# Retention and a gated feed-forward layer on one core: the same operations in another order

## The chip, the cores and the metric

The kernel runs on one core of a Trainium2 chip. The core has a matrix engine (PE, with its weight loads shown apart as PEld), a vector engine (DVE), a scalar engine (ACT), GpSimd (POOL) and a queue engine (SP), each working through its own list of instructions in order. They meet through semaphores. The metric is the time of one execution on the device in microseconds (us); runs are compared by their medians.

## The reference

Four sequences of 768 tokens, eight heads of 64. For each head a state is decayed by a fixed factor and takes up k times v at every token; the output is q times the state. What the eight heads give for a token is one row of 512, which is divided by its root mean square, multiplied by a gain, and goes through a gated layer with 1536 hidden units.

```python
gamma = 1.0 - 2.0 ** (-5.0 - np.arange(H))
for t in range(S):
    state = gamma * state + k[t] (outer) v[t]
    y[t] = q[t] @ state / sqrt(D)
x = y.transpose(0, 2, 1, 3).reshape(B * S, H * D)
xn = x / sqrt(mean(x * x) + 1e-6) * rms_g
out = (silu(xn @ w_gate) * (xn @ w_val)) @ w_out
```

## The kernel before, in words

The tokens of each sequence are cut into six chunks c of 128; b is one of the four batches. Inside a chunk the recurrence is written as matmuls: scores k times q for all pairs of tokens, multiplied by a mask that holds the decay and the causal order, times v, and for c > 0 also q times the state that the chunks before left. The four batches of a chunk are 512 tokens, and these go through the feed-forward layer together.

Nothing in the kernel is scheduled by the framework. A string, ORDER (lines 17 to 100), names every operation in the order in which it is written out, and the loop at its end (lines 600 to 604) calls one small function for each word. A word is an operation, its indices, after @ the engine (D, A, P, S for DVE, ACT, POOL, SP), and after / the PSUM banks that it writes (eight banks, 0 to 7). Each engine carries out its own instructions in this order; an instruction that waits holds up all that stand behind it on its engine. The words that matter here:

- Lq, Lk, Lv load a tile of 128 tokens (load, L314; for chunk 0 through POOL in an arrangement of eight tokens a row, L312). Through POOL the transfer also turns float32 into bfloat16; through SP it does not, and Cq, Ck, V make the bfloat16 tile later. wg, wv, wo load weights through POOL (L323, L330). These transfers of POOL use one software queue and eight semaphores in turn, so a POOL transfer waits for the one that was issued eight places before it. Loads of chunk 2 wait for the last piece of wo.
- Tq, Tk transpose with PE (L366, L371) and Eq, Ek copy the result out; from chunk 2 on tq, tk transpose by a DMA of SP (L387) instead. ident and pick are the matrices for this. J (L510) turns a transposed k of chunk 0 back.
- mk0, mk1, vd, yd, yt are exponentials on ACT that make masks and decays; mc (L282) makes the two halves of chunk 1's mask on POOL from the causal triangle.
- A are the scores (L403), M0 and M1 their products with the mask (DVE, L426), Y the output (L441, and L445 for the state's part), S its squares (ACT, L458), R the power -1/2 on POOL (L468, L470), N the normalised row xn (DVE, L482), X and XE its transposition (PE L495 with a copy, or SP's DMA L501 from chunk 2 on).
- D scales k (L517), K multiplies k and v (L526), U adds to the state in float32 (L534), B copies it to bfloat16 on POOL (st_b, L541), which the next chunk's Y reads.
- g and v are groups of the feed-forward layer's first matmuls (L549; c, blocks n0 to n1, batches b0 to b1), s the silu on ACT (L559), h the product on DVE (L567), d and, for the last tile, e the second matmuls (L574, L596), o the copy to SBUF, st the store by SP.
- G and GE spread the gain over the partitions (g_bc), tab loads ACT's table for silu, hot and H are idle matmuls (L234, L240) that only keep PE busy.

Buffers come from rings: a tile's slot is given again when its readers are done.

Of the kernel before, what the change touches and what calls it, by code (L numbers as in the profile page):

```python
# [27 lines left out]
s.0.3.4.0.3 XE.0.3@A g.0.0.4.3.4/6 s.0.2.3.0.3 h.0.0.2.1.2 g.0.4.6.3.4/4 wv.9.12 g.0.4.5.0.3/7 v.0.4.6.3.4/5
v.0.2.3.0.3/3 U.0.1@D s.0.4.6.3.4 Ek.1.1@A h.0.3.4.0.3 g.0.5.6.0.3/0 s.0.4.5.0.3 h.0.4.6.3.4 mc.0@P mc.1@P
v.0.4.5.0.3/5 v.0.0.4.3.4/7 h.0.2.3.0.3 Tk.1.2/1 g.0.6.7.0.4/4 Ek.1.2@A Lv.1.2@P h.0.4.5.0.3 g.0.7.8.0.4/2  # L30
Lv.1.0@P wo.0.4 Tq.1.2/1 s.0.5.6.0.3 s.0.7.8.0.4 Eq.1.2@D B.0.1 g.0.8.9.0.4/3 A.1.2/51 v.0.5.6.0.3/0 M1.1.2
wo.4.8 wo.8.12 s.0.0.4.3.4 v.0.7.8.0.4/2 h.0.0.4.3.4 h.0.5.6.0.3 h.0.7.8.0.4 Lk.1.3@P D.1.2@P Lk.2.0@S
v.0.6.7.0.4/7 Tk.1.0/0 M0.1.2 Lk.2.3@S Tq.1.0/6 v.0.8.9.0.4/1 s.0.6.7.0.4 Ek.1.0@A Eq.1.0@D h.0.6.7.0.4
s.0.8.9.0.4 Lq.2.1@S A.1.0/6042 M0.1.1 M1.1.0 B.0.2 M1.1.1 g.0.11.12.0.4/3 g.0.9.10.0.4/5 g.0.10.11.0.4/4
s.0.11.12.0.4 K.1.1/3 Y.1.1/0 s.0.10.11.0.4 h.0.8.9.0.4 S.1.1 U.1.1@D M0.1.0 v.0.9.10.0.4/2 v.0.10.11.0.4/3
R.1.1 v.0.11.12.0.4/4 s.0.9.10.0.4 K.0.3/7 h.0.9.10.0.4 D.1.0@P U.0.3@A Y.1.2/2 S.1.2 h.0.10.11.0.4 Y.1.0/3
N.1.1 h.0.11.12.0.4 Lq.1.3@P S.1.0 B.0.3 Lq.2.0@S Lk.2.1@S K.1.0/7 X.1.1/5 R.1.2 K.1.2/1 U.1.2@D d.0.3.0.4/0
N.1.2 R.1.0 N.1.0 d.0.0.0.4/6 XE.1.1@D d.0.1.0.4/4 d.0.2.0.4/2 X.1.0/5 d.0.3.4.8 X.1.2/1 d.0.0.4.8 Lv.1.3@P
d.0.1.4.8 XE.1.2@D d.0.1.8.12 U.1.0@D XE.1.0@A B.1.1 g.1.0.1.0.3/7 Tk.1.3/5 g.1.1.2.0.3/3 d.0.3.8.12 Tq.1.3/1
o.0.1@D Eq.1.3@D d.0.0.8.12 s.1.1.2.0.3 Ek.1.3@A o.0.3@A A.1.3/13 M1.1.3 Ck.2.0@A M0.1.3 tk.2.0 v.1.1.2.0.3/0  # L40
d.0.2.4.8 o.0.0@A Y.1.3/3 h.1.1.2.0.3 v.1.0.1.0.3/6 Ck.2.3@D S.1.3 R.1.3 Cq.2.1@D g.1.3.4.0.3/1 v.1.2.3.0.3/4
Lk.2.2@S d.0.2.8.12 tq.2.1 B.1.0 Ck.2.1@P Cq.2.0@P Lv.2.0@S s.1.0.1.0.3 s.1.3.4.0.3 tk.2.3 Lq.3.0@S N.1.3
X.1.3/0 g.1.2.3.0.3/1 s.1.2.3.0.3 XE.1.3@D v.1.3.4.0.3/7 h.1.0.1.0.3 Lq.2.2@S Cq.3.0@P Lk.3.0@S tq.2.0
g.1.8.9.0.4/6 o.0.2@A h.1.3.4.0.3 g.1.6.7.0.4/1 v.1.6.7.0.4/0 Ck.2.2@D g.1.7.8.0.4/5 tk.2.2 D.1.3@D
v.1.7.8.0.4/3 s.1.6.7.0.4 s.1.7.8.0.4 v.1.8.9.0.4/2 g.1.10.11.0.4/1 h.1.6.7.0.4 h.1.2.3.0.3 Lq.2.3@S B.1.2
Cq.2.2@P h.1.7.8.0.4 Cq.2.3@P s.1.8.9.0.4 g.1.11.12.0.4/3 h.1.8.9.0.4 s.1.10.11.0.4 tk.2.1 s.1.11.12.0.4
v.1.11.12.0.4/1 h.1.11.12.0.4 Lv.2.1@S st.0.1@S tq.2.2 v.1.10.11.0.4/4 h.1.10.11.0.4 V.2.0@A Ck.3.0@P
g.1.5.6.0.4/3 g.1.0.4.3.4/5 Lq.3.1@S s.1.0.4.3.4 s.1.5.6.0.4 g.1.4.5.0.4/2 A.2.0/5760 v.1.0.4.3.4/4 V.2.1@P
g.1.9.10.0.4/1 tq.2.3 Lv.2.3@S M1.2.0 M0.2.0 Y.2.0/3 M0.2.1 h.1.0.4.3.4 M1.2.1 v.1.9.10.0.4/7 s.1.9.10.0.4
s.1.4.5.0.4 K.1.3/4 v.1.4.5.0.4/0 S.2.0 U.1.3@D v.1.5.6.0.4/1 Cq.3.1@P h.1.9.10.0.4 R.2.0 h.1.4.5.0.4 A.2.2/5264  # L50
h.1.5.6.0.4 N.2.0 Y.2.1/7 Lk.3.1@S M0.2.3 M0.2.2 V.2.3@P B.1.3 S.2.1 d.1.1.0.10/1 K.2.0/3 tq.3.0 Ck.3.1@A
d.1.1.10.12 M1.2.3 R.2.1 M1.2.2 tk.3.0 Lv.2.2@S Y.2.3/6 S.2.3 V.2.2@P d.1.0.0.10/0 K.2.1/2 Y.2.2/5 tq.3.1
Lk.3.2@S S.2.2 N.2.1 R.2.3 d.1.2.0.12/7 R.2.2 U.2.1@D o.1.1@A XE.2.0@S Lk.3.3@S tk.3.1 K.2.3/4 N.2.3 U.2.0@D
N.2.2 Lq.3.3@S XE.2.1@S d.1.3.0.12/3 U.2.3@D A.3.0/2641 M1.3.1 d.1.0.10.12 XE.2.3@S XE.2.2@S M0.3.1 st.0.3@S
M0.3.0 st.0.2@S st.0.0@S B.2.1 Lv.3.1@S g.2.5.6.0.4/5 Lv.3.0@S o.1.3@A g.2.0.1.0.4/1 v.2.8.9.0.4/4 s.2.5.6.0.4
v.2.5.6.0.4/2 s.2.0.1.0.4 M1.3.0 Lq.3.2@S Lq.4.1@S Ck.3.3@D g.2.10.11.0.4/6 g.2.1.2.0.4/1 h.2.5.6.0.4 o.1.0@A
v.2.10.11.0.4/0 g.2.8.9.0.4/2 B.2.0 Cq.3.3@P s.2.10.11.0.4 Lk.4.0@S s.2.8.9.0.4 o.1.2@A g.2.6.7.0.4/5
v.2.0.1.0.4/6 Lk.4.1@S g.2.3.4.0.4/2 Ck.3.2@D h.2.0.1.0.4 v.2.3.4.0.4/7 v.2.6.7.0.4/6 Cq.3.2@D tq.3.3
g.2.11.12.0.4/3 V.3.1@A Cq.4.1@P s.2.6.7.0.4 Lv.3.2@S h.2.10.11.0.4 s.2.3.4.0.4 tk.3.3 Lq.4.0@S h.2.8.9.0.4
Lv.3.3@S K.3.1/2 s.2.1.2.0.4 h.2.3.4.0.4 tk.3.2 g.2.4.5.0.4/5 B.2.3 h.2.6.7.0.4 U.3.1@D V.3.2@D tq.3.2 Lq.5.0@S  # L60
st.1.0@S v.2.11.12.0.4/4 K.2.2/7 U.2.2@D s.2.11.12.0.4 Y.3.1/6 tq.4.1 st.1.2@S S.3.1 h.2.11.12.0.4 v.2.1.2.0.4/1
h.2.1.2.0.4 R.3.1 g.2.7.8.0.4/2 st.1.3@S v.2.7.8.0.4/4 Ck.4.1@P s.2.7.8.0.4 N.3.1 XE.3.1@S g.2.2.3.0.4/3
# [572 lines left out]
```

## Time and profile before

| what | us |
|---|---|
| three runs | 233.92 (median), 233.72, 234.96 |
| span of the profiled execution, first to last instruction | 233.6 |
| first feed-forward group starts on PE | 19.38 |
| last copy of a result starts on ACT | 230.50 |
| busy time: PE, DVE, ACT, POOL | 227.6, 130.4, 96.1, 89.7 |

For the profiled execution the span is its own time; what lies around it isn't in the profile. The profile comes from one execution. It has a page (busy times, the span in 40 slices, the chain of work that ended last, the costliest groups) and views in which one asks for instructions in order of time, groups by line, busy time by stretches, waits and transfers. A row of the timeline reads: start, length, engine, line, operation, what it writes <- what it reads, shape, count, and in brackets how long the engine stood idle before and what ended that. Where a row has a count, the instructions were merged, and the length is from the first's start to the last's end. The trace's durations of one engine's neighbours overlap a little.

### The profile page before, as it was taken

How to read it: one execution, taken by the hardware profiler on the slowest of the kernel's cores; microseconds unless marked ns; L12 is line 12 of the kernel's file. 1: busy time of each engine (PE TensorE's matmuls, PEld its weight loads, DVE VectorE, ACT ScalarE, POOL GpSimd, SP SyncE). 2: the span in 40 equal slices, each digit the busy share in tenths (PEclk: the TensorE clock that was granted, in tenths of full speed). 3: DMA queues.
4: the chain of work that ended last, by engine and by line, in shares of the span. 5: the costliest groups of instructions: out<-in, count | busy, mean ns of one | idle time of the engine just before them, and what ended most of it. 6: DMA issues, size and time to landing. Idle time of an engine off the chain costs nothing.

```text
span 233.6 us, 4637 instructions
## 1 busy us (share of the span) xinstructions
PE 227.6 (97%) x1771; PEld 120.8 (52%) x1771; DVE 130.4 (56%) x241; ACT 96.1 (41%) x231; POOL 89.7 (38%) x163
## 2 busy tenths in 40 slices
...
GB/s 126 147 180 123 127 179 184 205 145 215 133 206 214 171 194 140 262 218 221 235 173 146 179 221 206 198 149 142 148 61 27 112 0 0 3 90 9 83 89 93
DMA packets 105353, 33.61 MB, mean 144 GB/s; under 512 B 94449, under 2 KB 102385, under 8 KB 105330
## 3 DMA queue, kind: packets, MB, share of 16 engines
...
q8 instruction: 14, 0.23, 0.4%
...
## 4 chain that ended last, share of the span: by engine, by line
PE 89%; DMA 4%; POOL 2%; ACT 2%; DVE 1%; issue 0%; SPq 0%; POOLq 0%; DVEq 0%; ACTq 0%
PE v_ps L549 27%; PE g_ps L549 27%; PE o_ps L574 21%; PE a_ps L403 3%; DMA kb<-in_k_dram 3%; PE y_ps L441 2%; PE kv_ps L526 2%; PE y_ps L445 2%; DMA out_dram<-o_sb 1%; PE o_ps L596 1%; PE hot_ps L240 1%; PE t_ps L366 1%; PE t_ps L371 1%; PE xt_ps L495 1%; ACT xsq L455 1%; ACT xsq L458 1%
## 5 line engine op out<-in xcount | busy, mean ns | idle before, releaser
L567 DVE TENSOR_TENSOR hT<-sg,v_ps 128x512 bf16<-128x512 bf16 (+2 forms) x76 | 48.7, 656 | 47.8 <-PE v_ps L549 34.8
L549 PE MATMUL v_ps<-xnT,wv_b 128*128 128x512 bf16 (+2 forms) x344 | 71.2, 345 | 0.1
L559 ACT ACTIVATE sg<-g_ps 128x512 bf16<-128x512 f32 (+2 forms) x76 | 42.1, 575 | 70.6 <-PE g_ps L549 68.1
L549 PE MATMUL g_ps<-xnT,wg_b 128*128 128x512 bf16 (+2 forms) x344 | 70.0, 344 | 0.0
L574 PE MATMUL o_ps<-wo_b,hT 128*128 128x512 bf16 x276 | 63.5, 379 | 0.0
L549 PEld LDWEIGHTS <-wg_b 128*128 128x128 bf16 x344 | 30.4, 98 | 29.3
L549 PEld LDWEIGHTS <-wv_b 128*128 128x128 bf16 x344 | 30.2, 98 | 28.9 <-DVE am L426 0.6
L574 PEld LDWEIGHTS <-hT 128*128 128x128 bf16 x276 | 26.3, 98 | 29.1
L468 POOL TENSOR_SCALAR ms<-ssq 128x1 f32<-128x1 f32 x24 | 4.6, 190 | 59.1 <-ACT xsq L458 58.4
L426 DVE TENSOR_TENSOR am<-a_ps,causal 128x512 bf16<-128x512 f32 x32 | 20.6, 685 | 7.8 <-PE a_ps L403 7.5
L339 POOL TENSOR_TENSOR qb<-qf,ydec 128x512 bf16<-128x512 f32 x13 | 14.0, 1074 | 25.2 <-DMA qf<-in_q_dram 24.9
L146 ACT COPY o_sb<-o_ps 128x512 f32<-128x512 f32 (+1 forms) x16 | 8.8, 552 | 29.7 <-PE o_ps L574 23.1
L458 ACT ACTIVATE xsq<-y_ps 128x512 f32<-128x512 f32 x22 | 13.2, 599 | 18.9 <-PE y_ps L445 13.7
L482 DVE SCALAR_TENSOR_TENSOR xn<-y_ps,rstd,g_bc 128x512 bf16<-128x512 f32 x22 | 16.3, 748 | 4.3 <-POOL rstd L470 3.0
L146 DVE COPY o_sb<-o_ps 128x512 f32<-128x512 f32 (+1 forms) x10 | 6.4, 648 | 18.1 <-PE o_ps L574 12.2
L541 POOL CAST st_b<-st_f 64x256 bf16<-64x256 f32 x40 | 15.9, 398 | 1.3
L470 POOL TENSOR_TENSOR rstd<-ms,mhalf 128x1 f32<-128x1 f32 x24 | 13.3, 552 | 2.0
L534 DVE TENSOR_TENSOR st_f<-st_f,kv_ps 128x512 f32<-128x512 f32 x16 | 10.8, 684 | 5.2 <-PE kv_ps L526 4.6
L356 ACT ACTIVATE vp<-vf,vdec 128x64 bf16<-128x64 f32 x48 | 12.2, 343 | 0.0
L426 DVE TENSOR_TENSOR am<-a_ps,mask 128x512 bf16<-128x512 f32 x16 | 10.4, 686 | 2.5 <-PE a_ps L403 2.3
L240 PE MATMUL hot_ps<-one 128*128 128x512 bf16 x20 | 8.5, 547 | 1.1 <-DVE one L153 1.1
L441 PEld LDWEIGHTS <-am 128*128 128x128 bf16 x176 | 7.8, 99 | 3.1 <-issue 0.3
...
## 6 DMA issues: line engine op xcount, KB each, us to landing
...
```

What stands on the lines that cost most here:

```text
L146: (e.copy if e is ACT else e.tensor_copy)(out, in_)
L339: e.tensor_tensor(out=u["qb"], in0=u["qf"], in1=ydec[:, c, :, None].to_broadcast([128, H, D]), op=ALU.mult)
L426: DVE.tensor_tensor(out=u["am"][:, i], in0=u["a"][i], in1=m, op=ALU.mult)
L441: nc.tensor.matmul(y[:, h, :], u["am"][:, h % 2, h // 2, :], u["vp"][:, h, :], start=h == 0, stop=c == 0 and h == H - 1, skip_group_check= ...
L458: ACT.activation(xsq, flat(u["y"]), AF.Square, accum_out=u["ssq"])
L470: POOL.tensor_tensor(out=u["rstd"], in0=ms, in1=mhalf, op=ALU.pow)
L482: DVE.scalar_tensor_tensor(out=u["xn"], in0=flat(u["y"]), scalar=u["rstd"], in1=g_bc, op0=ALU.mult, op1=ALU.mult)
L541: POOL.tensor_copy(st_b[b][r, :, i * 64:i * 64 + 64], st_f[b][r, :, i * 64:i * 64 + 64])
L549: nc.tensor.matmul(p[:, (n - n0) * m:(n - n0 + 1) * m], W[w][0][:, s, n * 128:(n + 1) * 128], xnT[c][:, s, b0 * C:b1 * C], start=s == 0, s ...
L559: ACT.activation(sg[:, :cols], done["wg", c, n0, b0][:, :cols], AF.Silu)
L567: DVE.tensor_tensor(out=hT[c][:, n0:n1, b0 * C:b1 * C], in0=sg, in1=p, op=ALU.mult)
L574: nc.tensor.matmul(o_ps[c, b], hT[c][:, n, b * C:(b + 1) * C], wo_b[:, n, :], start=n == 0, stop=n == NFF - 1)
```

## The change

ORDER is replaced by another with the same operations. The making of pick, which was a part of the word ident, is a word of its own. Two things differ beside the order: some copies and scalings run on another engine (of q, k and v to bfloat16, of kT, qT and xnT out of PSUM, of the state and of the result), and banks are given out otherwise. The first loads through SP are k of (1,1), then k of (0,2); before it was the other way round. POOL's first transfers stand ahead of ident. The idle matmuls are as many, but two of them stand behind the last result.

The start of both strings, the place in chunk 0 and 1 that the prediction speaks of, and the end:

```diff
-H.8/3 yt Lk.0.2@S ident Ck.0.2@D vd Lk.1.1@S iota Tk.0.2/0 rms.1@S D.0.2@D Lk.0.0@P Lq.0.1@P H.3/1 Tk.0.0/2
-H.1/1 Tq.0.1/7 Ek.0.0@D mk1 hot.3/1 J.0.0/3 D.0.0@D mk0 Lq.0.0@P Lk.0.1@P Tq.0.0/6 Lq.0.2@P Eq.0.1@A Eq.0.0@A
-Tk.0.1/5 Ek.0.1@A Ek.0.2@D yd Lk.0.3@P H.1/1 Tq.0.2/4 tab Lq.0.3@P Eq.0.2@D hot.2/0 A.0.0/5017 M0.0.0 G/2 M1.0.0
-Tq.0.3/6 Lv.0.0@P M0.0.1 GE@A Tk.0.3/3 Eq.0.3@A Lv.0.1@P M1.0.1 Lv.0.2@P Lv.0.3@P wg.0.2 Y.0.0/4 wv.0.2 A.0.2/21
-wg.2.4 M1.0.2 Ek.0.3@A Lq.1.1@P H.3/0 A.0.3/61 S.0.0 M0.0.2 H.1/0 Y.0.2/3 K.0.0/0 J.0.1/5 M1.0.3 R.0.0 S.0.2
-N.0.0 M0.0.3 Y.0.1/1 H.1/2 X.0.0/4 J.0.3/7 wv.2.4 S.0.1 XE.0.0@D U.0.0@A R.0.2 R.0.1 Ck.1.1@A N.0.2 B.0.0 H.2/2
-Y.0.3/0 g.0.0.2.0.1/2 K.0.2/6 S.0.3 s.0.0.2.0.1 N.0.1 U.0.2@A wg.4.6 X.0.2/4 R.0.3 XE.0.2@D D.0.1@D
+Lk.1.1@S Lk.0.0@P H.1/0 Lk.0.1@P H.8/1 Lq.0.2@P Lq.0.1@P H.3/2 Lk.0.2@S Lq.0.0@P iota mk0 Lk.0.3@P Lq.0.3@P Lv.0.2@P
+ident pick Lv.0.0@P hot.2/3 Lv.0.1@P H.3/4 wg.0.2 Tk.0.0/5 Ck.0.2@A Lv.0.3@P wv.0.2 Tk.0.2/6 H.1/7 Tq.0.2/0 Tk.0.1/1
+vd mk1 D.0.2@D Eq.0.2@D Ek.0.2@D Tq.0.1/2 Tq.0.0/3 Ek.0.1@D A.0.2/47 hot.3/0 M1.0.2 Tk.0.3/6 M0.0.2 Ek.0.0@A wg.2.4
+Eq.0.1@A Eq.0.0@A yt A.0.0/5210 Tq.0.3/3 wg.4.6 H.1/7 Ek.0.3@A rms.1@S wv.2.4 M0.0.0 M1.0.0 Y.0.2/4 S.0.2 R.0.2 G/7
+Y.0.0/5 Eq.0.3@A A.0.3/62 M0.0.1 M1.0.1 Y.0.1/1 GE@A N.0.2 M0.0.3 M1.0.3 J.0.0/3 X.0.2/0 J.0.3/7 H.1/4 Y.0.3/6 wv.4.6
+S.0.0 yd R.0.0 S.0.1 N.0.0 R.0.1 N.0.1 XE.0.2@A J.0.1/2 X.0.0/0 g.0.0.2.2.3/4 X.0.1/5 K.0.2/1 wg.6.9 XE.0.0@D
+g.0.0.2.0.1/0 tab wv.6.9 D.0.1@D s.0.0.2.2.3 Lq.1.3@P Lq.1.2@P XE.0.1@D v.0.0.2.2.3/4 S.0.3 R.0.3 v.0.0.2.0.1/2
...
+Lq.1.1@P wv.9.12 X.0.3/4 Lk.1.2@P g.0.3.4.0.3/7 Lv.1.3@P wo.0.4 v.0.3.4.0.3/5 v.0.5.6.0.3/2 Lv.1.2@P Lv.1.1@P
...
+g.0.4.6.3.4/4 s.0.4.6.3.4 U.0.0@D g.0.8.9.0.4/7 v.0.6.7.0.4/5 v.0.4.6.3.4/0 wo.4.8 wo.8.12 h.0.4.5.0.3 h.0.5.6.0.3
+U.0.3@A D.1.0@P g.0.7.8.0.4/4 g.0.6.7.0.4/1 s.0.6.7.0.4 Tq.1.3/6 Lk.2.0@S s.0.7.8.0.4 v.0.7.8.0.4/2 Eq.1.3@D
+h.0.6.7.0.4 B.0.2 s.0.8.9.0.4 g.0.0.4.3.4/1 h.0.7.8.0.4 Ck.1.1@A v.0.8.9.0.4/6 h.0.8.9.0.4 h.0.4.6.3.4 s.0.0.4.3.4
+causal mc.0@P g.0.11.12.0.4/4 Tk.1.3/5 Ek.1.3@D s.0.11.12.0.4 Tk.1.0/2 Lq.2.0@S h.0.0.4.3.4 Tq.1.1/7 K.0.1/1 Tk.1.1/6
+Tq.1.2/0 Eq.1.2@D U.0.1@A A.1.3/45 Lk.2.3@S g.0.9.10.0.4/3 s.0.9.10.0.4 Ek.1.0@A Ek.1.1@A mc.1@P D.1.1@P Tq.1.0/1
+Eq.1.0@D Eq.1.1@D M0.1.3 v.0.9.10.0.4/0 h.0.9.10.0.4 Tk.1.2/3 M1.1.3 g.0.10.11.0.4/1 v.0.11.12.0.4/2 h.0.11.12.0.4
+A.1.0/7640 M1.1.0 M0.1.1 v.0.10.11.0.4/5 B.0.1 D.1.2@P B.0.3 Ek.1.2@A A.1.2/32 s.0.10.11.0.4 M0.1.0 Y.1.3/1 M1.1.1
...
-d.5.2.0.12/3 e.5.3.1/0 o.5.1@D st.4.2@S st.5.0@S st.5.1@S e.5.3.2/7 o.5.2@A st.5.2@S o.5.3.2@D st.5.3.2@S
-o.5.3.1@A e.5.3.0/5 st.5.3.1@S o.5.3.0@A st.5.3.0@S
+d.5.1.10.12 o.5.1@A st.5.1@S d.5.0.10.12 d.5.2.0.12/0 e.5.3.2/2 o.5.0@A e.5.3.1/3 o.5.3.2@D st.5.0@S o.5.2@A st.5.2@S
+o.5.3.1@D st.5.3.1@S st.5.3.2@S e.5.3.0/6 o.5.3.0@D H.2/7 st.5.3.0@S
...
     @op
     def ident_(e, bk):
         make_identity(nc, ident)
+
+    @op
+    def pick_(e, bk):
         DVE.tensor_copy(pick, ident.rearrange("p (s hp i) -> p i hp s", i=2, hp=NHP))
```

More of the change, by code (lines that the diff above doesn't have):

```diff
@@ L28 @@
[L28 to L62, printed above, removed]
@@ new lines @@
+M0.1.2 M1.1.2 d.0.1.0.4/6 d.0.0.0.4/4 S.1.3 R.1.3 d.0.3.0.4/7 N.1.3 Lk.2.2@S Lq.2.1@S K.1.1/0 U.1.1@D K.1.0/3
+h.0.10.11.0.4 B.0.0 U.1.0@D Y.1.0/2 Y.1.2/1 d.0.2.0.4/0 S.1.0 R.1.0 N.1.0 Y.1.1/5 S.1.1 R.1.1 N.1.1 K.1.2/3 d.0.3.4.8
+d.0.1.4.8 d.0.0.4.8 X.1.1/2 B.1.0 S.1.2 U.1.2@D X.1.0/5 R.1.2 N.1.2 XE.1.1@A X.1.3/3 Lq.2.3@S d.0.3.8.12 d.0.0.8.12
+X.1.2/2 d.0.1.8.12 XE.1.3@A XE.1.0@A XE.1.2@D v.1.7.8.0.4/1 g.1.7.8.0.4/3 D.1.3@P s.1.7.8.0.4 h.1.7.8.0.4 Lq.2.2@S
+Lk.2.1@S g.1.5.6.0.4/5 o.0.3@A K.1.3/2 U.1.3@D s.1.5.6.0.4 d.0.2.4.8 v.1.1.2.0.3/3 Cq.2.0@D Ck.2.0@P g.1.1.2.0.3/7
@@ new lines @@
+S.2.3 Lq.3.2@S N.2.0 R.2.3 tk.3.2 d.1.0.0.10/7 XE.2.1@S XE.2.0@S N.2.2 XE.2.2@S U.2.1@D d.1.1.0.10/2 N.2.3 XE.2.3@S
+d.1.2.0.12/4 U.2.2@D st.0.0@S Lv.3.3@S g.2.11.12.0.4/1 s.2.11.12.0.4 o.1.3@A Lk.4.0@S Ck.5.2@D V.3.0@A g.2.1.2.0.4/0
+v.2.11.12.0.4/3 Cq.3.1@D Cq.3.2@D Lv.5.2@S tq.3.1 g.2.3.4.0.4/1 s.2.3.4.0.4 g.2.0.1.0.4/6 Lk.3.3@S Lk.4.3@S tq.3.0
+Lq.4.1@S Cq.4.0@D h.2.11.12.0.4 s.2.0.1.0.4 Ck.4.0@D v.2.0.1.0.4/3 h.2.0.1.0.4 v.2.3.4.0.4/1 h.2.3.4.0.4 U.2.3@D
+d.1.0.10.12 v.2.6.7.0.4/6 g.2.6.7.0.4/3 s.2.6.7.0.4 s.2.1.2.0.4 tk.3.0 o.1.2@A v.2.1.2.0.4/1 h.2.1.2.0.4 st.0.1@S
```

88 lines of the change are left out of this document (50 added, 38 removed).

## The prediction

> **What bounds the kernel now.** I read the page's first line, then the busy time by stretches, then the instructions in order of time, engine by engine.
>
> ```profile
> span 233.6 us, 4637 instructions
> ```
>
> ```profile
> 0.00:19.38 19.38, 16.77 (x228) 9.11 (x229) 12.88 (x49) 13.35 (x31) 14.74 (x31) 0.91 1.33 154
> 19.38:140.00 120.62, 120.62 (x966) 66.86 (x964) 73.59 (x123) 49.90 (x119) 62.43 (x104) 1.00 1.06 186
> 140.00:170.00 30.00, 29.76 (x237) 15.10 (x232) 20.36 (x34) 14.21 (x43) 9.52 (x21) 1.00 0.83 172
> 170.00:230.50 60.50, 60.46 (x357) 29.74 (x355) 23.57 (x37) 18.30 (x42) 2.96 (x8) 1.00 0.15 46
> 230.50:233.60 3.10, 0.00 (x0) 0.00 (x0) 0.00 (x0) 0.32 (x1) 0.00 (x0) 1.00 0.27 85
> ```
>
> The columns after the length are busy us of PE, PEld, DVE, ACT and POOL. From 19.38 to 230.5 PE rests for 0.3 us in all, at full clock. What an order can still win lies in front of 19.38, where the first feed-forward group starts, and in 3.1 us of last copy and store. What it can lose lies everywhere. The start, on PE and on POOL:
>
> ```profile
> 6.73 0.44 PE L366 MATMUL t_ps<-pick,kb 128*64 128x64 bf16 x16 [0.43 <-DMA kb<-in_k_dram]
> 9.75 0.44 PE L366 MATMUL t_ps<-pick,kb 128*64 128x64 bf16 x16 [1.01 <-DMA kb<-in_k_dram]
> ...
> 19.38 0.61 PE L549 MATMUL g_ps<-xnT,wg_b 128*128 128x128 bf16 x8
> ```
>
> ```profile
> 1.00 0.24 POOL L168 IOTA row_i<- 128x128 int32 x1
> ...
> 2.08 0.76 POOL L312 DMA_DIRECT2D kb<-in_k_dram  x1
> 2.83 1.05 POOL L312 DMA_DIRECT2D qb<-in_q_dram  x2
> 3.85 0.82 POOL L312 DMA_DIRECT2D kb<-in_k_dram  x1
> ...
> 6.17 3.59 POOL L314 DMA_DIRECT2D vp<-in_v_dram  x4
> ...
> 15.16 0.19 POOL L468 TENSOR_SCALAR ms<-ssq 128x1 f32<-128x1 f32 x1 [2.04 <-ACT xsq L458]
> 15.43 0.58 POOL L470 TENSOR_TENSOR rstd<-ms,mhalf 128x1 f32<-128x1 f32 x1
> ```
>
> PE waits twice for k from POOL's queue, passes other waits with idle matmuls (L240), and has its first group when batch 0 is normalised, transposed and copied.
>
> **The change part by part.** The instructions are the same but for the engine of some copies. Ahead of the first feed-forward group both orders do the same PE work: eight transpositions of q and k, the scores of four batches, the gain row, four y, three J; before then has K and X of batch 0, after has X of batches 2 and 0, all groups of four matmuls. The idle matmuls are as many, but two (H.2) now stand behind the last result, where they run beside the last store and cost nothing. So the start's gain is the first group's time, read against 19.38. I walk there with durations of the rows.
>
> ```profile
> 2.95 1.66 ACT L277 ACTIVATE qdec<-row_f,qbias,lngp 128x128 f32<-128x128 f32 x4 [0.88 <-DVE qbias L191]
> 4.74 2.44 ACT L269 ACTIVATE mask<-row_m,nbias 128x128 f32<-128x128 f32 x8
> ...
> 8.78 0.59 ACT L146 CAST qT<-t_ps 128x512 bf16<-128x512 f32 x1 [0.28 <-PE t_ps L366]
> ...
> 17.18 0.60 ACT L458 ACTIVATE xsq<-y_ps 128x512 f32<-128x512 f32 x1 [2.12 <-PE y_ps L441]
> ...
> 7.22 0.69 DVE L146 CAST kT<-t_ps 128x512 bf16<-128x512 f32 x1 [1.66 <-PE t_ps L366]
> ...
> 11.61 2.48 DVE L426 TENSOR_TENSOR am<-a_ps,mask 128x512 bf16<-128x512 f32 x4
> 17.24 0.74 DVE L482 SCALAR_TENSOR_TENSOR xn<-y_ps,rstd,g_bc 128x512 bf16<-128x512 f32 x1
> ```
>
> POOL: the first transfer follows row_i at 1.3 instead of 2.08, so the software queue starts 0.8 us sooner. Five transfers (0.76, 0.82 and three of 0.53) end at 4.5, row_m, a short select, at 4.8, two more transfers at 5.9, the first vp at 6.8, and the identity, now behind all of these, at 7.4; DVE's pick at 7.6. PE has done its opening idle matmuls before that, so the first transposition waits for pick until 7.7, a loss of 1 us against 6.73. But now k and q have landed, and five 16-matmul groups (0.37 apart from start to start), one of four and one idle matmul run through to 10.1, where before the fourth transfer held PE until 9.75 and three such groups were still to come. DVE makes qT and kT of batch 2 by 10.05 (0.69, and less for the second, whose source is bfloat16); the scores run to 10.5 and 11.7; six products of 0.62 (2.48 / 4) end at 14.4. ACT, with eight exponentials from 4.8 and a copy between, is free at 8.2, copies two or three tiles to 10.8, makes qdec (1.66) until 12.5, copies kT (0.5 to 0.6), squares y of batch 2 (0.6 and its readout) until 13.6, copies qT and g_bc until 14.7. POOL: from 7.4 eight further transfers, three vp of 0.9 and five of weights at 0.8 (row 29.84, below), end at 14.1; ms and rstd (0.8) at 14.9. This is where weights stand ahead of the first power: rstd could have been there at 14.4, but xn needs g_bc as well, at 14.7, so they cost 0.2 us. DVE: xn of batch 2 (0.74) to 15.6, two products to 16.9, xn of batch 0 to 17.6. PE transposes it to 17.8, and the first group starts at 17.9. **Start: 1.5 us won.** Bounds: 0.7 if the transfers land no sooner than before (0.8 less), 2.1 if PE keeps its full clock and ACT's copies meet no wait.
>
> Weights behind the start. Of the software queue:
>
> ```profile
> 20.50:22.50 2.00, 2.00 (x37) 1.94 (x35) 1.96 (x5) 1.56 (x5) 1.84 (x5) 1.00 0.38 27
> 22.50:30.00 7.50, 7.50 (x85) 5.75 (x84) 4.70 (x9) 3.10 (x7) 7.48 (x11) 1.00 1.27 138
> 30.00:40.00 10.00, 10.00 (x91) 5.59 (x90) 6.55 (x11) 3.94 (x8) 9.33 (x13) 1.00 1.74 183
> ...
> 29.84 0.83 POOL L323 DMA_DIRECT2D wv_b<-in_moe_w_val_dram  x1
> DMA to landing us min/median/max: 10.7/10.7/10.7
> ```
>
> The last column is GB/s. Before, POOL issued too late and the queue ran dry from 20.5 (27 against 183 GB/s); the last of wv_b landed at 29.84 + 10.7 = 40.5. Now sixteen transfers are out by 14.1 and the queue stays full: 2.0 x 156 + 7.5 x 45 = 650 KB, over 183, is 3.6 us, and with the 0.8 it lands at about 36. Nothing on PE waited for weights before (row 19.38:140.00), so this alone wins nothing.
>
> But it is paid on POOL. An issue there waits for the landing of the transfer eight places ahead:
>
> ```profile
> 38.05 0.89 POOL L314 DMA_DIRECT2D kb<-in_k_dram  x1 [0.55 <-DMA wg_b<-in_moe_w_gate_dram]
> 39.01 1.04 POOL L517 TENSOR_TENSOR kd<-kb,vdec 128x512 bf16<-128x512 bf16 x1
> 40.00 0.85 POOL L541 CAST st_b<-st_f 64x256 bf16<-64x256 f32 x2
> ...
> 30.62 2.12 POOL L282 TENSOR_TENSOR mask<-causal,vdec 128x512 f32<-128x512 bf16 x2
> ...
> 62.63 0.23 PE xt_ps L495 x4
> ...
> 65.89 0.86 PE v_ps L549 x4
> ```
>
> In the new order the third wo transfer stands eight behind that last wv_b, and behind it, in POOL's order, stand D.1.0, B.0.2, causal, both mask halves, D.1.1, B.0.1, D.1.2, B.0.3: 36 + 0.75 issue + 3 x 1.04 + 3 x 0.85 + 0.3 (causal, a select) + 2.1 = 44.8 for the end of B.0.3, the state of batch 3. The second half of Y.1.3 on PE reads it. PE work from the first group to there: all 24 group-equivalents of the chunk's feed-forward (0.865 each, 20.8 us), fourteen small groups of 0.23 (3.2), three scores (1.3), half a y (0.2): 25.5, so PE is there at 17.9 + 25.5 = 43.4. **A wait of 0 to 2 us; I take 1.0**, as the queue is likelier a little quicker than that mean rate. What follows on POOL (rstd of batch 3, B.0.0) slides with PE. DVE's products that need the masks stand at 39.8 and 41, the masks are there at 40 and 41: no cost, or part of the same wait.
>
> The middle and the end. Bank for bank I compared the PE work between a tile's last writer and the next user of its bank; the shortest distances before (0.65 for scores, 0.86 for groups, 0.9 for K) cost nothing in row 19.38:140.00, and the new ones (1.1, 0.9, 1.1) are no shorter, but for one o tile at 0.86 (1.4), worth 0.1. The last three pieces end as before with a 192-column copy, on DVE instead of ACT, and a store: 0. **Sum: 233.6 - 1.5 + 1.0 = 233.1.** The three runs have their median 0.3 above the profiled span: **233.4 us**.
>
> **The rivals.** (1) *The start's gain is kept*: B.0.3 comes in time, because the queue moves faster than my mean. For it: wv_b need land only 1.4 us sooner than 36, and 183 GB/s is a mean over transfers of several shapes. Against it: a chain of nine POOL instructions without slack. Then 233.4 - 1.0 = 232.4, to 231.9 if the start wins 2.1.
>
> (2) *Slower: SP's queue becomes the bound.*
>
> ```profile
> 114.54 2.88 SPq L314 DMA_DIRECT2D vf<-in_v_dram  x3
> ...
> L501 SPq DMA_TRANSPOSE xnT<-xn x16: 1188/1216/1842, 83.3 to 183.2; - x16
> ...
> 50.77 1.01 SPq L314 DMA_DIRECT2D kf<-in_k_dram  x2
> ```
>
> SP starts on chunk 2 when wo has landed, and then works nearly without rest. Up to the transposed xn of chunk 3's last batch (XE.3.3) the old order has 34 loads, 25 transposes and 8 stores, the new one 40, 28 and 6. With 0.96 a load (2.88 / 3), 1.25 a transpose and 0.5 a store that is 38.4 + 35 + 3 = 76.4, from about 48.5 (wo some 2 us sooner than when it let SP go, 50.8): 124.9, landed at 126.3. PE wants it at 127.5 (17.9, 108.6 of PE work counted in the same way, and the 1.0 at Y.1.3). The slack is 1.2 us: PE waits from 0.99 us a load on, and at 1.04 it waits 40 x 0.08 - 1.2 = 2.0 us: 235.4. For it: the same holds for kT of chunk 3 (A.3.2) and qT of chunk 5. Against it: before, SP stood idle for some 4 us in this stretch.
>
> (3) *The half clock falls later.* PE ran at half rate again:
>
> ```profile
> 11.04:14.26 3.22, 3.22 (x60) 0.77 2.31 162
> 14.26:19.38 5.12, 5.07 (x66) 0.81 1.65 189
> ```
>
> The number before the last two is the granted clock: (0.23 x 3.22 + 0.19 x 5.12) x 2 = 3.4 us at half rate, in a time of waits that hid most of it. The new order moves PE's waits; if the same stretch falls behind 17.9, on dense groups, it costs 3.4 / 2 = 1.7 us: 235.1. Against it: in the new walk PE waits less between 7.7 and 12.5 than before. [...]
>
> (4) *The transfers land no sooner*: the new order isn't ahead where it says. The two kf loads on SP's queue move until about 5 (issued at 0.8 and 1.3, the second landing 3.8 later):
>
> ```profile
> DMA to landing us min/median/max: 3.0/3.4/3.8
> ```
>
> The software queue now starts inside that time. If it gains nothing by it, the start wins 0.8 less: 234.2. [...] Here only 0.8 us of overlap is at stake.
>
> **How the numbers follow.** Forecast, a start gained and partly given back, 233.4 (232.8 to 234.2): 0.37. Gain kept, 232.4: 0.28. SP late, 235.4: 0.23. Clock, 235.1: 0.06. No sooner, 234.2: 0.06. The bound of 0.5% (about what a measurement of this kernel can tell from no change) is 1.2 us: below 232.75 or above 235.1. Faster: 0.26 of the kept gain and 0.04 of the forecast's low end, 0.30. Slower: 0.20 of SP's case, 0.03 of the clock's, 0.02 of the forecast's tail, 0.25. Same: 0.45. The range runs from 231.9 (start 2.1 won, no wait) to 235.8 (SP's case at 1.05 us a load), and leaves out about 0.1 on either side.
>
> **What would show it.** The first feed-forward group at 17.9 (right from 17.3 to 18.4); no stretch of the software queue under 100 GB/s between 15 and 45; PE idle before L445 near 43.5 with POOL's st_b named as releaser, for about 1 us; wo landed before 49.5; after it PE as dense as in row 19.38:140.00. Wrong would be: the first group after 19; no wait at Y.1.3; or PE waits for kT, qT or xnT over 1 us in all, which would be rival 2, and its place in SP's order would tell which transpose.

## The result, and the profile after

The changed kernel takes 240.68 us (median of four runs, 239.89 to 241.35), the kernel before 233.84 (four runs, 233.72 to 234.96): 1.028 times as long (95% interval 1.024 to 1.032), far outside the range of the prediction. The profiled execution took 241.23; its page begins with a span 5.8 us longer than the 233.6 of before:

```profile
span 239.4 us, 4635 instructions
```

PE's busy time by stretches; after the length come busy us of PE, PEld, DVE, ACT and POOL, then the granted clock, the DMA share and GB/s:

```profile
0.00:17.29 17.29, 15.00 (x225) 8.52 (x226) 11.90 (x47) 12.82 (x30) 15.81 (x33) 1.00 1.34 166
...
43.65:44.74 1.09, 0.00 (x1) 0.00 (x0) 1.09 (x3) 0.00 (x0) 0.98 (x3) 1.00 1.25 209
44.74:127.99 83.25, 83.25 (x628) 44.59 (x627) 54.17 (x86) 34.22 (x87) 31.42 (x59) 1.00 0.95 188
127.99:131.80 3.81, 0.15 (x1) 0.03 (x1) 1.72 (x3) 0.00 (x0) 1.19 (x2) 1.00 0.48 96
131.80:136.53 4.73, 4.73 (x15) 1.82 (x16) 0.00 (x0) 0.60 (x1) 0.00 (x0) 0.64 0.98 240
...
163.94:168.23 4.29, 3.37 (x17) 1.30 (x15) 2.96 (x6) 0.59 (x1) 0.87 (x1) 1.00 0.59 85
```

The first feed-forward group starts at 17.29, 2.1 earlier than in the first profile of before. Then PE loses 1.1 us (43.65 to 44.74), 3.7 (127.99 to 131.80), 1.7 by half clock right behind that (4.73 x 0.36), and 0.9 (163.94 to 168.23): 7.4 together. The waits of PE by what ended them (us in all, times, longest):

```profile
PE v_ps L547 <- DMA xnT<-xn: 3.7, 1, 3.7
...
PE y_ps L443 <- POOL st_b L539: 1.1, 1, 1.1
```

The long one is for xnT of chunk 3. Its last piece (XE.3.3) is a transposing DMA of SP. On DVE the last two of the normalised rows are ready at 123.5:

```profile
122.09 1.41 DVE L480 SCALAR_TENSOR_TENSOR xn<-y_ps,rstd,g_bc 128x512 bf16<-128x512 f32 x2 [0.47 <-POOL rstd L468]
```

SP's rows, the first of its list and the last before the wait ends, show when the transposes go out:

```profile
47.62 0.39 SPq L312 DMA_DIRECT2D kf<-in_k_dram  x1
...
115.46 2.56 SPq L312 DMA_DIRECT2D vf<-in_v_dram  x2
118.06 1.77 SPq L385 DMA_TRANSPOSE kT<-kb  x1
119.88 1.22 SPq L312 DMA_DIRECT2D qf<-in_q_dram  x2
121.14 1.79 SPq L385 DMA_TRANSPOSE kT<-kb  x1
123.03 2.17 SPq L499 DMA_TRANSPOSE xnT<-xn  x1
125.32 1.20 SPq L385 DMA_TRANSPOSE kT<-kb  x1
126.61 3.83 SPq L499 DMA_TRANSPOSE xnT<-xn  x3
```

In these last rows SP goes from one item to the next without a rest. XE.3.3 is the last of the final three: issued from 129.23 to 130.44 (in the merged row, 126.61), 5.7 us after its input was there. The chain of work (start, length, what) goes through it into PE:

```profile
129.23 2.44 DMA xnT<-xn
131.67 0.14 issue
131.80 1.02 PE v_ps L547 x4
```

So far this is the prediction's second rival, with a price of 3.7 + 1.7 and not 2.0.

### The profile page after: what moved, and what is told of

Its sections match the earlier page's. It is cut to its first block, busy times and chain, and to the rows that moved or that the text cites. A ratio compares the mean times of both kernels' runs of the same rounds, so it can differ in the third digit from the quotient of the medians.

```text
span 239.4 us, 4635 instructions
## 1 busy us (share of the span) xinstructions
PE 228.5 (95%) x1771; PEld 121.1 (51%) x1771; DVE 133.2 (56%) x244; ACT 94.0 (39%) x224; POOL 87.8 (37%) x160
## 4 chain that ended last, share of the span: by engine, by line
PE 79%; POOL 11%; DVE 3%; DMA 2%; issue 2%; ACT 1%; POOLq 0%; DVEq 0%; ACTq 0%; SPq 0%
PE g_ps L547 25%; PE v_ps L547 24%; PE o_ps L572 21%; DMA xnT<-xn 2%; PE y_ps L443 2%; PE kv_ps L524 2%; PE a_ps L401 2%; PE y_ps L439 2%; POOL vp L312 1%; POOL kd L515 1%; POOL st_b L539 1%; POOL rstd L468 1%; PE o_ps L594 1%; DVE xn L480 1%; PE xt_ps L493 1%
## 5 line engine op out<-in xcount | busy, mean ns | idle before, releaser
L565 DVE TENSOR_TENSOR hT<-sg,v_ps 128x512 bf16<-128x512 bf16 (+2 forms) x76 | 48.2, 656 | 50.1 <-ACT sg L557 26.9
L547 PE MATMUL g_ps<-xnT,wg_b 128*128 128x512 bf16 (+2 forms) x344 | 72.3, 349 | 0.4 <-DMA xnT<-xn 0.4
L539 POOL CAST st_b<-st_f 64x256 bf16<-64x256 f32 x40 | 17.2, 430 | 18.9 <-DVE st_f L532 10.2
L141 DVE COPY o_sb<-o_ps 128x512 f32<-128x512 f32 (+2 forms) x10 | 5.8, 582 | 21.6 <-PE o_ps L572 11.7
L141 ACT COPY o_sb<-o_ps 128x512 f32<-128x512 f32 x16 | 9.2, 584 | 20.5 <-PE o_ps L572 17.7
L356 POOL TENSOR_TENSOR vp<-vf,vdec 128x512 bf16<-128x512 f32 x8 | 8.7, 1088 | 21.9 <-DMA vf<-in_v_dram 21.9
L337 POOL TENSOR_TENSOR qb<-qf,ydec 128x512 bf16<-128x512 f32 x7 | 7.2, 1041 | 17.5 <-DMA qf<-in_q_dram 17.5
L354 ACT ACTIVATE vp<-vf,vdec 128x64 bf16<-128x64 f32 x40 | 10.1, 340 | 0.0
```

The source lines that it names most:

```text
L141: (e.copy if e is ACT else e.tensor_copy)(out, in_)
L539: POOL.tensor_copy(st_b[b][r, :, i * 64:i * 64 + 64], st_f[b][r, :, i * 64:i * 64 + 64])
L547: nc.tensor.matmul(p[:, (n - n0) * m:(n - n0 + 1) * m], W[w][0][:, s, n * 128:(n + 1) * 128], xnT[c][:, s, b0 * C:b1 * C], start=s == 0, s ...
L565: DVE.tensor_tensor(out=hT[c][:, n0:n1, b0 * C:b1 * C], in0=sg, in1=p, op=ALU.mult)
```

## Experiments

*Theory S*: SP's list in front of XE.3.3 is too long, and from its first load on it sets the landing, whatever PE has won before; the wait then costs the clock. *Rival R*: the normalised rows come too late from DVE and POOL, and SP's place doesn't matter. *Rival C*: the half clock comes by itself. *Rival A*: PE's waits simply add up. Of the list's pace: *Q*, SP's own items set it, or *T*, the transfer engines, which both queues use (the page of the kernel before gives SP's queue 50.2% and POOL's 30.1% of the span of 16 engines). Each diff shows the words of the one engine concerned, in its order; the runs of before beside them have medians of 233.9 to 234.3.

**Once more the kernel before (before_again)**, unchanged.

> The kernel before once more, for a second profile of it. Its first profile has a span of 233.6 at a mean clock of 0.993; the runs timed since have spans of 231.4 to 232.9, most at 1.00. If the half clock of the first profile (12.8 to 16.2, in the start) is what made it longer, this one, at full clock, has its first feed-forward group at about 17.9 instead of 19.38, a span near 232.1 and the same density after it; then the start of the changed kernel (17.3) wins about 0.6 against a usual execution and not 2.0. If the start was not it, the first group stays at 19.4 and the 1.5 us lie elsewhere.

233.72 us in the run. First its page, then two rows of PE in order of time, the first feed-forward group and the first group of chunk 3.

```profile
span 231.7 us, 4613 instructions
```

Its PE:

```profile
17.06 0.61 PE L549 MATMUL g_ps<-xnT,wg_b 128*128 128x128 bf16 x8
...
126.99 1.89 PE L549 MATMUL g_ps<-xnT,wg_b 128*128 128x512 bf16 x7
```

At full clock (1.00 up to there) the old start reaches its first group at 17.06, not 19.38 and not the 17.9 that I expected. From there to the last copy it takes 211.5 us, the first profile 211.1. So the first profile was of an execution with half clock in its start (0.50 from 12.80 to 16.21), 1.9 us longer than this one. It was not the usual one: of the 55 executions of the kernel before that were timed beside these runs, six have a mean granted clock of 0.993 or less, as the first profile has, and the median span is 232.2. **The changed start wins nothing; it is 0.2 us later** in this pair. Between executions the first group moves by more than that: 17.06 here and 17.72 in before_dose (below), which has the old start too, 17.27 to 17.65 in the eight profiles with the changed start. Measured from here the changed kernel is 7.7 us longer, and the account closes: 0.2 + 7.4, and 0.1 more from the last matmul to the end.

**The transposes of xn first on SP (xn_first), and half of that (xn_half).**

```diff
-tk.4.0 Lq.4.2@S Lq.5.1@S tk.4.1 XE.3.1@S tk.4.2 XE.3.2@S XE.3.0@S XE.3.3@S Lk.5.3@S
+Lq.4.2@S XE.3.1@S tk.4.0 XE.3.2@S XE.3.0@S XE.3.3@S Lq.5.1@S tk.4.1 tk.4.2 Lk.5.3@S
```

That is xn_first; xn_half has:

```diff
+Lq.4.2@S tk.4.1 XE.3.1@S tk.4.2 XE.3.2@S XE.3.0@S XE.3.3@S tk.4.0 Lq.5.1@S Lk.5.3@S
```

> The changed kernel with SP's list alone reordered: XE.3.1, XE.3.2, XE.3.0 and XE.3.3 (the transposed xn of chunk 3) go ahead of the load Lq.5.1 and the transposes tk.4.1 and tk.4.2, and tk.4.0 goes behind XE.3.1. Theory S (SP's list is too long in front of them): xn of the last batch is ready at 123.5, its transpose lands at about 126.7 and not at 131.7, PE reaches the group at 127.8 or so without a wait, the 3.7 us and the half clock behind it (1.7) go: about 235.3. Rival R (the normalised batches themselves come too late from DVE and POOL): the wait stays within 1 us of 3.7, about 240.5. Rival C (the half clock comes by itself, not from the wait): the wait goes and 1.7 us of half clock stay, about 237.

> The changed kernel with half of that: only Lq.5.1 and tk.4.0 go behind XE.3.3. Theory S: 1.8 + 0.5 and their gaps less in front, the wait falls from 3.7 to about 1.3; whether a wait of that length still costs the clock is open: 238 without, 240 with. Rival R: wait and time as in the changed kernel.

xn_first: 239.25 (237.51 to 240.27), 1.021 of before (1.015 to 1.027). xn_half: 241.52 in one run. PE's rows of xn_first that have a wait:

```profile
129.14 1.02 PE L547 MATMUL v_ps<-xnT,wv_b 128*128 128x512 bf16 x4 [0.99 <-DVE vp L356]
...
147.72 0.62 PE L401 MATMUL a_ps<-qT,kT 64*128 64x128 bf16 x16 [0.86 <-DMA qT<-qb]
152.67 0.38 PE L524 MATMUL kv_ps<-vp,kb 128*128 128x128 bf16 x4 [0.72 <-ACT sg L557]
...
166.82 1.02 PE L547 MATMUL g_ps<-xnT,wg_b 128*128 128x512 bf16 x4 [0.85 <-DMA xnT<-xn]
```

And in xn_half:

```profile
130.66 1.02 PE L547 MATMUL v_ps<-xnT,wv_b 128*128 128x512 bf16 x4 [2.60 <-DMA xnT<-xn]
```

Both lists shorten the wait: 3.7 with five other items in front of XE.3.3 in this part, 2.6 with three, 1.0 with two. (The last is put down to a DVE product, but XE.3.3 landed at about 129.1: issued at 126.64, 2.4 from issue to landing.) The size for three items isn't clean. In xn_half's execution two transposes far in front of the changed place took 2.33 and 2.36 us (tk.3.3, tq.4.0), not 1.24 and 1.48 as in the changed kernel, so by an estimate about 2 of its 2.6 are not due to the place. R falls by xn_first, and C by both: no half clock in either (mean granted clock 1.00 in both, 0.992 in the changed kernel). But xn_first gains only 1.4 us where I forecast 5.4, and xn_half, forecast at 238 or 240, gains nothing, because the next items of the same list are late now: PE comes sooner to the scores of chunk 4 and waits for qT, and to K.4.3, whose bank is freed by a silu behind V.5.1. ACT's row of xn_half shows that one, a scaling of v that nobody needs yet, waiting for its load:

```profile
152.07 2.02 ACT L354 ACTIVATE vp<-vf,vdec 128x64 bf16<-128x64 f32 x8 [3.33 <-DMA vf<-in_v_dram]
```

In the changed kernel the same scaling starts at 151.47 without a wait, and PE doesn't wait between 136 and 160: the long wait had given SP time to catch up. Moving items about within a list that is too long moves the wait.

**The same surplus put into the kernel before (before_dose).** (Lq.5.2 also goes ahead of XE.3.0.)

```diff
-Lv.4.2@S XE.3.0@S Lq.5.2@S XE.3.2@S XE.3.3@S Lk.4.2@S Lq.4.2@S Lv.5.3@S tk.4.0 tk.4.1 tq.4.0 Lv.4.3@S Lk.4.3@S Lq.4.3@S
+Lv.4.2@S Lk.4.2@S Lq.5.2@S Lq.4.2@S tk.4.0 Lv.5.3@S tk.4.1 Lv.4.3@S tq.4.0 Lk.4.3@S Lq.4.3@S XE.3.0@S XE.3.2@S XE.3.3@S
```

> The kernel before with SP's list alone changed: six loads (Lk.4.2, Lq.4.2, Lv.5.3, Lv.4.3, Lk.4.3, Lq.4.3) and three transposes (tk.4.0, tk.4.1, tq.4.0) that stood behind XE.3.3 go ahead of XE.3.0, the same surplus that the changed kernel has there. Theory S: 6 x 0.85 + 3 x 1.3 + gaps is 9.5, less 2.8 that SP rests there now: XE.3.3 lands at about 133 and not at 126.5, PE (at 128.9) waits about 4 us and then loses up to 1.7 by half clock: about 239 (237.5 to 240.5). Rival R: SP's list isn't what counts, within 1 us of 233.8.

242.63 (242.01 to 243.06), 1.036 of before (1.033 to 1.039). PE's first group of chunk 3:

```profile
133.06 3.57 PE L545 MATMUL g_ps<-xnT,wg_b 128*128 128x512 bf16 x8 [5.26 <-DMA xnT<-xn]
```

Two stretches behind that, in the columns of above:

```profile
131.91:135.30 3.39, 2.24 (x6) 0.87 (x7) 0.00 (x0) 0.34 (x1) 0.00 (x0) 0.50 0.73 181
135.30:138.70 3.40, 3.40 (x10) 1.17 (x8) 0.00 (x0) 0.86 (x2) 0.00 (x0) 0.50 0.01 3
```

SP's list alone makes such a loss in the old order (8.3 us), with nothing else of the change: the landing is where I put it (133), the wait 5.3, and half clock lasts 6.8 us. I was 3.6 us low: PE came at 127.8 and not at the first profile's 128.9, and half clock lasted 6.8 us and not 3.4.

**The wait filled with idle matmuls (fill).** 17 of them, 128x512, stand on PE where the changed kernel waits for xnT of chunk 3.

```diff
+H.17/3
 v.3.6.7.0.4/3
```

> [...] The wait is filled, not shortened. If the half clock after it comes from the wait: no stretch of half clock near 133, 1.7 us less, about 239.0. Rival C (it comes by itself): the clock falls all the same, about 240.7.

240.14 (239.13 to 240.89), 1.025 of before (1.020 to 1.029). PE's rows there:

```profile
128.31 3.83 PE L235 MATMUL hot_ps<-one 128*128 128x512 bf16 x17
133.49 1.02 PE L547 MATMUL v_ps<-xnT,wv_b 128*128 128x512 bf16 x4 [1.35 <-DMA xnT<-xn]
134.35 1.03 PE L547 MATMUL g_ps<-xnT,wg_b 128*128 128x512 bf16 x4
```

And one of SP's:

```profile
108.37 2.43 SPq L385 DMA_TRANSPOSE kT<-kb  x1
```

With PE kept busy the clock stayed full (1.00 in the stretches from 127.00 to 138.00, four matmuls in 0.86). The mean granted clock of the four executions says the same: 0.992 or 0.993 in all four of the changed kernel, 0.999 or 1.00 in three of the four with idle matmuls and 0.993 in the other, which has no profile. So here the half clock came from the rest, not by itself. The time shows little of it: in this execution SP's list ran late with nothing changed in front (this transpose, tk.3.3, took 2.43 instead of 1.24, the next, tq.4.0, 2.48 instead of 1.48), and xnT landed 1.7 us later. So the price of the clock, 1.7, is read from the changed kernel's own row, not from this median.

**A gain in front of the wait (kd_late).** POOL's words:

```diff
-D.1.1@P B.0.1 D.1.2@P B.0.3
+D.1.1@P B.0.1 B.0.3 D.1.2@P
```

> The changed kernel with one POOL instruction moved: D.1.2, a product of 1.04 us that nobody needs before 51, goes behind B.0.3. B.0.3 ends at 43.7 instead of 44.7 and PE's wait of 1.1 us at 43.5 goes. Theory S (from SP's first load at 47.6 on, SP's list sets the time at which xnT of chunk 3 lands, whatever PE has won before): PE comes 1.1 us sooner to the same landing at about 131.7 and waits 4.8 there instead of 3.7; time as in the changed kernel, 240.7 (240.0 to 241.4). Rival A (waits add up): 1.1 less, 239.6.

240.83 (240.20 to 242.82), 1.028 of before (1.025 to 1.031). PE hardly waits at Y.1.3 any more, and at chunk 3:

```profile
132.30 1.86 PE L547 MATMUL v_ps<-xnT,wv_b 128*128 128x512 bf16 x4 [4.94 <-DMA xnT<-xn]
```

PE comes 0.8 sooner (127.36, against 128.14 in the changed kernel) and waits 1.3 longer. A falls by this row. By the time it does so only just: 1.1 less than the changed kernel's 1.028 is 1.023, a little below the interval. This execution is the longest of the four (242.82): two of its transposes (tk.3.3, tq.4.0) were slow as in xn_half, the landing came 0.5 later than in the changed kernel, and half clock lasted 6.8 us (0.50 from 130.65 to 137.50). The other three took 240.20 to 241.28. The wait that I had forecast at 43 was there, and taking it away won the whole nothing.

**Fewer items in front (defer), and four of them in another queue (k_on_pool).**

```diff
-Lv.5.2@S
...
-Lq.5.2@S
...
-Lq.5.1@S
...
 Lv.5.1@S
+Lq.5.2@S Lq.5.1@S Lv.5.2@S
```

That is defer. k_on_pool, and the same for batches 1, 2 and 3:

```diff
-Lk.4.0@S
+Lk.4.0@P
...
-Ck.4.0@D
```

> The changed kernel with three loads of chunk 5 (Lv.5.2, Lq.5.2, Lq.5.1) moved behind Lv.5.1, to where SP rests for 5 us now; all transposes stay in their order. Theory S: 3 x 0.9 to 1.0 less ahead of XE.3.3, the wait falls from 3.7 to about 0.9 and costs no clock: 4.5 won. But ACT's V.5.1 (scaling v by 8 products, 2.0 us) stands in front of the silu that frees the bank of K.4.3 and waits for its load: that comes 2.9 sooner, PE 4.5 sooner, so 1 to 1.6 us are given back near 150: about 237.5. Rival R: no change, 240.7.

> The changed kernel with the four k loads of chunk 4 moved from SP's queue to POOL's, which casts them on the way (four casts on DVE, POOL and ACT fall away). Theory Q (SP's own list of items sets the pace): four items of 0.83 + 0.06 less ahead of XE.3.3, 3.5 us, the wait at 128 falls from 3.7 to about 0.3, no half clock; 1 us given back near 150: about 236.5. Theory T (the transfer engines, which both queues share, set it): the landing doesn't move, 240 to 241.

defer: 236.54 (236.22 to 237.95), 1.012 of before (1.008 to 1.015): 4.1 us back for three loads. k_on_pool: 238.07 (237.36 to 240.82), 1.018 (1.012 to 1.023). SP's last three transposes of xn in defer end with XE.3.3, and PE's first group of chunk 3 follows (its wait is put down to a DVE sum, but XE.3.3 lands just before it starts):

```profile
122.79 4.76 SPq L499 DMA_TRANSPOSE xnT<-xn  x3
...
128.85 1.02 PE L547 MATMUL v_ps<-xnT,wv_b 128*128 128x512 bf16 x4 [0.73 <-DVE st_f L532]
```

In k_on_pool:

```profile
92.78 3.35 SPq L385 DMA_TRANSPOSE qT<-qb  x1
...
125.62 3.84 SPq L499 DMA_TRANSPOSE xnT<-xn  x3
```

XE.3.3 is out at 127.55 in defer, 2.9 sooner than in the changed kernel (130.44): 0.96 us a load, and the wait was 0.7. In k_on_pool it is out at 129.46, 1.0 sooner for four loads, and PE's wait there is 1.0, not 0.3. While three of the k loads in POOL's queue were on their way (issued from 88.6 to 91.0, landed 3.7 to 6.5 later), SP's transpose at 92.78 took 3.35, against 1.70 in the changed kernel. PE got a new wait at 92.7 for xnT of chunk 2:

```profile
94.46 1.89 PE L547 MATMUL g_ps<-xnT,wg_b 128*128 128x512 bf16 x8 [1.74 <-DMA xnT<-xn]
```

The time lies between Q (236.5) and T (240 to 241). One execution of each isn't enough to divide the pace between SP and the transfers; the rows fit a part of both.

**Weights behind the first power (powers_first).** POOL's words:

```diff
-wg.4.6 wv.2.4 R.0.2 wv.4.6 R.0.0
+R.0.2 wg.4.6 wv.2.4 wv.4.6 R.0.0
```

> The changed kernel with two of the weight transfers (wg.4.6, wv.2.4) behind the first power (R.0.2) instead of ahead of it. The power's input is ready at 13.2 and POOL is busy with transfers until 13.4, so the first rstd comes 0.3 us sooner, but xn needs the row of g at 14.1 as well: the first group 0.2 sooner, 17.1. Theory S: no change of the whole (240.7), since the wait at 128 takes it back. If weights ahead of the power were the cause of the loss, the time would fall by some us.

244.06 in one run. POOL's rows:

```profile
13.25 0.19 POOL L466 TENSOR_SCALAR ms<-ssq 128x1 f32<-128x1 f32 x1 [1.30 <-ACT xsq L456]
13.52 0.58 POOL L468 TENSOR_TENSOR rstd<-ms,mhalf 128x1 f32<-128x1 f32 x1
14.06 0.83 POOL L321 DMA_DIRECT2D wg_b<-in_moe_w_gate_dram  x1
14.88 1.50 POOL L321 DMA_DIRECT2D wv_b<-in_moe_w_val_dram  x2
16.46 0.19 POOL L466 TENSOR_SCALAR ms<-ssq 128x1 f32<-128x1 f32 x1
```

PE's first group:

```profile
18.36 0.61 PE L547 MATMUL g_ps<-xnT,wg_b 128*128 128x128 bf16 x8
```

I was wrong here. The first power comes 0.3 sooner, but POOL stood idle for 1.3 to get it, and the transfers now hold up the second power by 1.2: the first group is 1.1 later and SP's first load 0.6 later. xnT of chunk 3 is 1.6 later, with half clock for 6.8 us (0.50 from 132.59 to 139.40) instead of 3.4; up to 1.3 of that may come from two transposes that are slow here too (tk.3.3 1.98, tq.4.0 2.06). So the 244.06 need not be the price of the powers alone. What the rows show is that the start gains nothing by it: the weights ahead of the first power are not the cause of the loss.

**All waits taken away (mended, mended_pick, mended_all).** mended is xn_first and defer together, with Lv.5.3 deferred too, and:

```diff
@@ POOL @@
-D.1.1@P B.0.1 D.1.2@P B.0.3
+B.0.1 B.0.3 D.1.1@P D.1.2@P
...
-B.4.0 B.4.2 R.4.2 B.4.3 R.4.3 R.4.1
+R.4.2 R.4.1 R.4.3 B.4.0 B.4.2 B.4.3
@@ DVE @@
-N.4.2 N.4.3 N.4.1 U.4.1@D h.3.11.12.0.4
+N.4.2 N.4.1 N.4.3 h.3.11.12.0.4 U.4.1@D
@@ ACT @@
-V.5.1@A
...
 o.3.1@A
+V.5.1@A
```

> The changed kernel with its waits taken away together: on SP the loads Lv.5.2, Lq.5.2, Lq.5.1, Lv.5.3 behind Lv.5.1, and tk.4.1 and tk.4.2 behind XE.3.3, tk.4.0 behind XE.3.1; on POOL D.1.1 and D.1.2 behind B.0.3, and R.4.1 and R.4.3 ahead of the casts B.4.0, B.4.2, B.4.3; on DVE N.4.1 ahead of N.4.3 and the last product of chunk 3 ahead of U.4.1; on ACT V.5.1 behind the copy o.3.1. Theory S: the start's 2.0 us are kept, 1.1 at 43.5, 3.7 at 128, 1.7 of half clock and some 1.3 near 165 go: span 239.4 - 7.8 = 231.6 to 232.5, time 232.5 to 233.5, 0.3 to 0.8% under the kernel before. If something else holds the changed kernel (the order of banks on PE, the software queue), it stays above 236.

233.84 (ten runs, 233.14 to 234.95), 0.999 of before (0.997 to 1.001). Its page:

```profile
span 231.6 us, 4609 instructions
```

PE's first groups of chunks 3 and 4:

```profile
126.55 1.03 PE L547 MATMUL v_ps<-xnT,wv_b 128*128 128x512 bf16 x4
...
160.53 1.02 PE L547 MATMUL g_ps<-xnT,wg_b 128*128 128x512 bf16 x4 [0.41 <-DMA xnT<-xn]
```

All 6.8 us are back with nothing but the order changed, so no other cause of that size is left in the new order. The forecast of 232.5 to 233.5 was missed, as it still held 2.0 us won in the start: without waits both spans are the same (231.6 and 231.7), so the start is worth nothing against the usual old one. Two more tries at the start on top of it: ident and pick ahead of four of POOL's transfers, with two idle matmuls left out (mended_pick); and in addition wv.2.4 behind R.0.2, wv.4.6 behind R.0.1 (mended_all).

> The mended order, and in its start the identity and DVE's pick two steps earlier on POOL, ahead of four transfers, with two of the idle matmuls on PE left out. PE's first transposition waits for pick until 7.4 now; q of batch 2 lands at 7.2, so scores and products come 0.5 to 1.0 sooner: first group at 16.6, and as nothing behind it waits for SP any more, the whole is 0.5 to 1.0 shorter than the mended 233.84: 233.1. If the start's gain were lost behind it again, as in the changed kernel, no change.

> The mended order with the early pick, and on POOL one weight transfer less ahead of each of the first powers (wv.2.4 behind R.0.2, wv.4.6 behind R.0.1). With the early pick the sum for the first power is ready at 12.9, but POOL issues wv.2.4 until 13.4, so the pick gained nothing: first group 17.24. Now the first rstd comes 0.5 sooner, the second 0.5, the first group at about 16.75; the software queue keeps enough in it that no weight lands later than it is needed. If the start counts as long as nothing behind it waits for SP: 233.3 (0.5 less than 233.85). If a weight is missed, PE waits near 24 for wv_b and the time stays.

233.85 (0.998 of before, 0.996 to 1.000) and 234.04 (1.002, 1.000 to 1.004). POOL's first power in mended_pick:

```profile
13.46 0.19 POOL L466 TENSOR_SCALAR ms<-ssq 128x1 f32<-128x1 f32 x1
```

PE's first group in mended_all, and its next wait:

```profile
16.84 0.61 PE L547 MATMUL g_ps<-xnT,wg_b 128*128 128x128 bf16 x8
...
22.09 1.41 PE L547 MATMUL v_ps<-xnT,wv_b 128*128 128x128 bf16 x12 [0.46 <-DVE xn L480]
```

The early pick won 0.4 on PE, and POOL, busy with transfers until then, took it back (its power at 13.46 as before). With those moved the first group came at 16.84, as expected, and the 0.45 went at 22, where xn of batch 3 is late. mended_pick is nominally 0.2% ahead of the kernel before and mended 0.1%, at the edge of what these runs can tell or below it. Both forecasts, 233.1 and 233.3, were missed.

## Why the prediction was wrong

- *What bounds the kernel now*: right, PE from its first group on.
- *Start, 1.5 us won*: the walk was right to 0.6 us (17.29 measured, 17.9 forecast; the first rstd at 14.4, forecast 14.9; the weights ahead of it cost 0.3, forecast 0.2). **The first step that failed is what it was read against: 19.38, from an execution with half clock in its start.** I had the rows (0.77 and 0.81) and priced that stretch only for the new order. The old start at full clock has 17.06: 0.2 lost, not 1.5 won. The 0.3 between span and run was wrong for the same reason: in the executions for which both are known they are 1.7 to 2.3 apart, so the first profile, at 233.6, was over 1 us longer than the usual one.
- *Weights*: right. The last wv_b landed at 35.6 (forecast 36), SP's first load went out at 47.6 (48.5).
- *The wait of 1.0 at Y.1.3*: right in size (1.1), but it doesn't count (kd_late).
- *The middle, 0*: **this is the step that cost the result.** It was rival 2, and its mechanism was right: the last transposed xn of chunk 3, PE there at 128.1 (forecast 127.5). Its size was off. SP needed 82.8 us for the 74 items (47.62 to 130.44), not 76.4. By kind, with the gaps between items: forty loads about 35.4 (forecast 38.4), 28 transposes 40.8 (35.0), six stores 3.6 (3.0), rests 3.0 (0). Half of the transposes' surplus is gaps of about 0.1 that I left out; the other half is their length, 38.0 in all. Twenty-one of them took 1.19 to 1.30 and seven 1.48 to 2.17, six of these right behind two or more loads, and I had used little more than the median. SP's rests I had counted as a reserve against the rival, when a list that waits for its producers rests in the new order too.
- *The half clock* (rival 3) was given as a case by itself, and that PE's waits bring it was my estimate; no run had shown it. Here it came with rival 2: behind the wait of 3.7 it fell on dense groups (0.50 from 133.10 to 136.50), and with that wait filled but for 1.35 the clock stayed at 1.00 (fill). Its forecast price, 1.7, was right; it was not added to rival 2's.
- *The end, 0*: right to 0.1. Left out of the sum were 0.9 near 165, where N.4.1 and the last product of chunk 3 are late on DVE.

Against the usual old execution (span 231.7) the measured terms are 0.2 for the start, 1.1 at Y.1.3, 3.7 and 1.7 in the middle, 0.9 near 165 and 0.1 at the end: 239.4. The forecast had -1.5 for the start, 1.0 at Y.1.3 and nothing for the rest, on a base of 233.6.

What stays open is how far SP and how far the transfers set the list's pace, and why some executions take 1 to 2 us more for the same transposes.
